# Gated sum of linear and softmax attention on one core: a new written-out order, later transposing loads, TensorE transposes in the last set, and split rings

## The chip, the cores and the metric

The kernel runs on one core of one Trainium2 chip. That core has TensorE (matmuls; PE in the profile, its weight loads PEld), VectorE (DVE), ScalarE (ACT), GpSimd (POOL) and SyncE (SP), which only issues DMA transfers here. The engines run beside each other and wait for each other with semaphores. The metric is the device time of one execution in microseconds (us); lower is better.

## What is computed

The input x has 2048 rows of 512 values. Branch A is linear attention with a learned feature map, branch B is plain softmax attention; both have 32 heads of 16. A sigmoid gate g mixes the two results row by row. Cut from the reference (weights `wqkv`, `w_phi`, `wo` are given per branch):

```python
# branch A
pq = einsum("bhsd,hdf->bhsf", q, w_phi);  pk = einsum("bhsd,hdf->bhsf", k, w_phi)
phi_q = concat([softmax(pq), softmax(-pq)]);  phi_k = concat([softmax(pk), softmax(-pk)])
kv = einsum("bhsf,bhsd->bhfd", phi_k, v);  z = einsum("bhsf->bhf", phi_k)
a = (einsum("bhqf,bhfd->bhqd", phi_q, kv) / (einsum("bhqf,bhf->bhq", phi_q, z)[..., None] + 1e-6)) @ wo_A
# branch B
p = softmax(einsum("bhqd,bhkd->bhqk", q, k) * 16 ** -0.5)
b = einsum("bhqk,bhkd->bhqd", p, v) @ wo_B
# gate
g = sigmoid((x * gate_w).sum(-1, keepdims=True));  out = g * a + (1 - g) * b
```

Branch B holds most of the work: 32 heads x 2048 x 2048 exponentials.

## The kernel before, in words

**Tiling.** x is held transposed in `xT` (512 channels on 4 x 128 partitions, 2048 columns). Branch B goes through 32 *sets*: a set is 512 query rows and 4 heads (8 heads share a group `g`, and `par` takes one half of them). In a set, each of the 16 key tiles `kt` (128 keys) gives two pieces of scores of 128 x 1024. TensorE makes each piece with two `qk` matmuls (L1067) into two of the seven PSUM banks of the ring `B_r`; the eighth bank, `psO`, gathers the result.

**Two engines take the exponentials.** Most key tiles go to ACT, which takes one piece of 128 x 1024 per instruction (L1077) into a buffer of the ring `E_r` (10 buffers). The others go to DVE, which makes an integer whose bits are an approximate exponential: four instructions of 128 x 512 (L1082) into part 0 of a buffer `T`, and then two *shifts* of 128 x 2048 (L1091) into parts 1 and 2 of the same buffer. A buffer of the ring `T_r` (3 of them) is thus one allocation of three parts. TensorE adds an ACT tile to `psO` with one `pv` round (four matmuls of 512 columns side by side, two for each piece, L1106), and a DVE tile with three rounds, whose weights are scaled copies of the values (`vB`, `vS`). Only tiles in `DSET` may go to DVE; of the last `ND(s)` (5) of them the planner decides one by one, during planning, to which engine each goes (`alt`, `choose`).

**After a set,** DVE empties `psO` into `OT` (L741), SP transposes it with a DMA (L1124) into `OTT`, DVE divides by the sums (L1128, L1129), and after two sets SP transposes the result (L1136) into `oBT`. The very last set uses four TensorE transposes (L1119) for the first of these steps and the DMA of L1136 for the second. The output projection (L1151) multiplies `oAT` and `oBT` by the two output weights; for the last 512 rows its last matmul is kept apart (L1156), since it needs the last set. DVE (L1167) or ACT (L1164) scales by 1 - g, and SP stores (L1170).

**Branch A and the projections** run in between: q, k and v of group g before its first set (L758, L813), the gate (L856, one-column matmuls), `Wp` (L874), sums of squares for a range check (`sumsq`, L886 and L889), and the feature map (`phi`) with its GpSimd sums (L946 to L956).

**What sets the order.** Nothing above is issued in the order of the source. `_build` records every operation with its engine, a priority (`st_(x)` is set number x on a nominal clock), a cost in us and its buffers (`add`). `_Sched.run` then plays these operations through a list scheduler, on the author's machine: at each step it places the operation that can start earliest, and on TensorE it weighs the next `qk` against other ready work with some tolerances (`_pick_pe`). `style(seed)` draws these tolerances, and the table `STYLES` holds one seed for each stretch of `WINDOW` us of the planned time. The result is one fixed list of instructions for each engine; each engine runs its list strictly in turn, and waits for semaphores where the plan says so. The planner's prices are fixed numbers: 0.905 for an ACT piece, 0.6 for a DVE instruction of L1082 or L1091, 5.0 for the issue of the transposing load `wat`.

**The start.** x arrives in two ways. Columns 0 to 1023 of `xT` come from two plain loads (`x_in`, L687) into `T` buffers, which TensorE transposes (L773) and ACT and DVE copy (L740, L741). Columns 1024 to 2047 come from two transposing DMA loads (L698). A third transposing load, `wat` (L700), brings a transposed weight.

Of the kernel before, what the change touches and what calls it, by code (L numbers as in the profile page):

```python
# [15 lines left out]
D = 512  # L16
# [12 lines left out]
DSET = (5, 7, 9, 11, 13, 15)  # L29
# [8 lines left out]
WINDOW = 20.0  # L38
STYLES = (0, 61504, 30715, 62437, 20893, 99383, 94218, 0, 0, 75239, 0, 42781, 82966, 0, 0, 54421, 94168, 4721, 53470, 5563, 49382, 0, 0, 57337, 54423, 7875, 0, 7940, 59810, 78070, 3529, 35308, 31287, 0, 22189, 0, 0, 16999, 0)
# [32 lines left out]
class _Op:  # L72
    __slots__ = ("eng", "fn", "occ", "lat", "prio", "deps", "tiles", "mode", "name", "dma", "lane", "kind",
                 "n_open", "users", "start", "end", "count", "sem", "vc", "seq", "est", "run", "alt", "frees")


class _Sched:
# [114 lines left out]
    def _pick_pe(self, cands, free, pend, last_mode):  # L192
# [3 lines left out]
        def due(o):  # L196
            return self.load(o.run, free, pend) - 0.5
# [17 lines left out]
        over = CONT if bc[1].kind == "cont" else (t - bc[1].est - PVS) if bc[1].kind == "pv" else min(t, self.nom) - bc[1].prio  # L215
# [185 lines left out]
def _general(fast):
# [197 lines left out]
def _build(ctx, nc, A_x, A_wqkv, A_w_phi, A_wo, B_wqkv, B_wo, gate_w, out):  # L599
# [100 lines left out]
    op_wat = add("sp", -90, 5.0, lambda e: e.dma_start_transpose(WAT[:], A_wqkv[:, 0:2 * D]), name="wat", dma=7.0)  # L700
# [549 lines left out]
```

## Time and profile before

| | |
|---|---|
| median of 3 runs | 773.16 us (772.70 to 773.52) |
| the profiled execution: its own time | 773.7 us |
| the same execution: span from first to last instruction | 771.8 us |
| busy in the span | ACT 710.9, DVE 703.8, PE 693.0, POOL 191.7 us |
| mean granted TensorE clock | 0.988 |
| exponentials | ACT 720 pieces (L1077); DVE 608 + 304 instructions (L1082, L1091) |

The span is 1.9 us shorter than the time of the same execution. A PE that is busy is not a PE at its peak, because matmuls overlap. An instruction's idle time stands in brackets with what ended it. In the views by stretches each engine has its busy time, with the number of instructions in brackets.

### The profile page before, as it was taken

Reading aid. Unit: us, or ns where it says so; the run is one execution under the profiler, and the core shown is the slowest. Engines: PE = TensorE matmul, PEld = TensorE weight load, DVE = VectorE, ACT = ScalarE, POOL = GpSimd, SP = SyncE. Lnnn points to the kernel's source line nnn. Section 1 sums busy time; section 2 is a strip of 40 time slices with the busy share of each in tenths; the row PEclk is TensorE's granted clock in tenths of the full one; section 3 lists DMA queues with packets and bytes.
Section 4 is the critical chain, followed back from the end, with each engine's and each line's share of the span. In section 5 each row is a group of like instructions: output and inputs, shape, how many; then the busy total and the mean of one; then the engine's idle time right before and its main releaser. Section 6 shows DMA issues by size and latency. Waiting matters only on the chain.

```text
span 771.8 us, 15551 instructions
## 1 busy us (share of the span) xinstructions
PE 693.0 (90%) x6390; PEld 218.9 (28%) x6452; DVE 703.8 (91%) x1228; ACT 710.9 (92%) x796; POOL 191.7 (25%) x226
## 2 busy tenths in 40 slices
PE   6999999999989999898999989998988998988883
PEld 3333333233323222232232222222222232222221
DVE  2887899999999999999999999999999999999991
ACT  3998798989999999999999999999999999999990
POOL 5216231233343432422232021222221121200000
PEclk9999899999999999999999999999999999999997
DMA  9200000001010000002122021120211211100001
GB/s 235 39 15 8 8 14 16 15 29 49 8 23 1 8 15 15 14 14 29 41 56 50 22 35 42 29 39 17 47 24 35 49 42 35 32 19 8 14 8 39
DMA packets 72702, 23.92 MB, mean 31 GB/s; under 512 B 64560, under 2 KB 72624, under 8 KB 72624
## 3 DMA queue, kind: packets, MB, share of 16 engines
q1 hardware_dynamic: 71568, 22.58, 13.8%
q8 instruction: 53, 0.87, 0.5%
q10 hardware_dynamic: 1056, 0.26, 0.2%
q14 instruction: 25, 0.20, 0.1%
HBM read 4.21 MB, written 2.10 MB: 8 GB/s over the span
## 4 chain that ended last, share of the span: by engine, by line
ACT 43%; PE 27%; DVE 24%; DMA 3%; SPq 1%; issue 1%; ACTq 0%
ACT E L1077 41%; DVE T L1082 13%; PE psR L1067 11%; PE psO L1106 7%; DVE T L1091 6%; PE psR L758 4%; PE psR L1151 2%; DMA OTT<-OT 2%; PE psR L813 1%; SPq L700 1%; ACT WAT L940 1%; DVE ob L1129 1%; DVE OT L741 1%; DMA oAT<-WAv 1%; DVE WAv L1167 1%
## 5 line engine op out<-in xcount | busy, mean ns | idle before, releaser
L1077 ACT ACTIVATE E<-psR 128x1024 bf16<-128x1024 f32 x720 | 678.1, 1057 | 30.2 <-PE psR L1067 21.0
L1082 DVE TENSOR_SCALAR T<-psR 128x512 int16<-128x512 f32 x608 | 387.9, 681 | 21.1 <-PE psR L1067 18.7
L1067 PE MATMUL psR<-qz,kT 64*128 64x512 bf16 x2048 | 348.5, 385 | 44.2 <-ACT E L1077 29.0
L1091 DVE TENSOR_SCALAR T<-T 128x2048 int16<-128x2048 int16 x304 | 199.4, 691 | 3.0
L1067 PEld LDWEIGHTS psR<-qz,kT 64*128 64x128 bf16 x2048 | 86.5, 93 | 301.8 <-ACT E L1077 179.3
L1106 PE MATMUL psO<-E,vB 128*18 128x512 bf16 x1440 | 132.0, 384 | 1.7 <-ACT E L1077 0.8
L1106 PE MATMUL psO<-T,vS 128*18 128x512 bf16 x1216 | 105.4, 383 | 0.5
L1106 PE MATMUL psO<-T,vB 128*18 128x512 bf16 x608 | 59.8, 384 | 1.5 <-DVE T L1082 1.3
L946 POOL TENSOR_TENSOR WAT<-WAT 128x512 f32<-128x512 bf16 x16 | 18.5, 1154 | 166.4 <-DVE T L1091 140.5
L1106 PEld LDWEIGHTS psO<-E,vB 128*18 128x18 bf16 x1440 | 33.0, 88 | 61.7 <-issue 41.5
L951 POOL TENSOR_TENSOR tr<-WAT 128x256 f32<-128x256 f32 x32 | 23.3, 728 | 79.3 <-DVE T L1091 79.3
L1106 PEld LDWEIGHTS psO<-T,vS 128*18 128x18 bf16 x1216 | 26.7, 87 | 57.4 <-DVE T L1091 26.6
L956 POOL TENSOR_TENSOR phk<-phk,ss 128x1024 bf16<-128x1024 bf16 x16 | 31.0, 1935 | 47.7 <-DVE T L1091 47.7
L956 POOL TENSOR_TENSOR WAT<-WAT,ss 128x1024 bf16<-128x1024 bf16 x16 | 30.9, 1928 | 46.3 <-DVE T L1091 46.3
L758 PE MATMUL psR<-xT,WB 128*128 128x512 bf16 x108 | 28.5, 380 | 4.1 <-issue 2.3
L758 PE MATMUL psR<-Wp,xT 128*128 128x512 bf16 x106 | 28.4, 380 | 3.4 <-issue 2.9
L946 POOL TENSOR_TENSOR WAT<-phk 128x512 f32<-128x512 bf16 x16 | 18.9, 1180 | 41.2 <-DVE T L1091 41.1
L741 DVE CAST OT<-psO 128x512 bf16<-128x512 f32 x32 | 21.8, 683 | 6.4 <-PE psO L1106 6.3
L1106 PEld LDWEIGHTS psO<-T,vB 128*18 128x18 bf16 x608 | 14.7, 87 | 31.3 <-issue 22.3
L826 POOL TENSOR_SCALAR vS<-vB 128x288 bf16<-128x288 bf16 x24 | 10.4, 433 | 51.1 <-DVE T L1091 48.4
L1129 DVE TENSOR_TENSOR ob<-OTT,rB 128x256 bf16<-128x256 bf16 x31 | 18.7, 604 | 0.2
L940 ACT ACTIVATE WAT<-psR 128x512 bf16<-128x512 f32 x32 | 18.3, 637 | 0.3 <-PE psR L758 0.3
(103 smaller groups left out, 372.2 us busy)
## 6 DMA issues: line engine op xcount, KB each, us to landing
qz<-qst SPq DMA_DIRECT2D x120, 16.0 KB, 1.8
out_dram<-WAv SPq DMA_DIRECT2D x12, 128.0 KB, 1.9
WB<-in_B_wqkv_dram SPq DMA_DIRECT2D x3, 384.0 KB, 6.7
T<-in_A_x_dram SPq DMA_DIRECT2D x2, 512.0 KB, 4.3
WAv<-in_A_wqkv_dram SPq DMA_DIRECT2D x1, 512.0 KB, 5.1
WB<-in_A_wo_dram SPq DMA_DIRECT2D x1, 512.0 KB, 3.5
WB<-in_B_wo_dram SPq DMA_DIRECT2D x1, 512.0 KB, 3.4
out_dram<-Wp SPq DMA_DIRECT2D x4, 128.0 KB, 3.8
```

The lines of the kernel that those rows point to most:

```text
L741: return add("dve", prio, 0.6, lambda e: e.tensor_copy(dst(), src()), deps=deps, tiles=tiles, name=name)
L758: calls = [lambda e, t=t: e.matmul(tile.ap[:, off:off + 512], lhsT=lhs(t), rhs=rhs(t), start=(t == 0), stop=(t == KT - 1)) for t in range(KT)]
L940: ex = [add("act", prio, 0.48, lambda e, s=s: e.activation(ev()[:, :, 16 * s:16 * s + 16], P(), ACTF.Exp, scale=1.0 - 2.0 * s), deps=[f] + ...
L946: p1 = pool(prio + 2, 1.23, lambda e: e.tensor_tensor(v8(), eg()[:, :, 0:8], eg()[:, :, 8:16], ALU.add), ex + use_wat, tiles=[ee, tr], nam ...
L951: p2 = pool(prio + 2, 0.92, lambda e: e.tensor_tensor(u4(), v8()[:, :, 0:4], v8()[:, :, 4:8], ALU.add), [p1], tiles=[tr, tr2])
L956: return pool(prio + 6, 1.95, lambda e: e.tensor_tensor(eg(), eg(), ss.ap[:, 1, :].unsqueeze(2).to_broadcast([128, 64, DH]), ALU.mult), [o ...
L1067: ins = e.matmul(rs[h].ap, lhsT=kT[64 * h:64 * h + 64, g, 128 * kt:128 * (kt + 1)], rhs=qt.ap[64 * h:64 * h + 64, c, :], start=True, stop= ...
L1077: exps.append(add("act", pr + 0.5 * cc, 0.905, lambda e, rs=rs, E=E: e.activation(E.ap.rearrange("p (a n) -> p a n", n=512), pair(rs), ACT ...
L1082: exps.append(add("dve", pr + 0.5 * cc + 0.01 * h, 0.6, lambda e, rs=rs, T=T, cc=cc, h=h: e.tensor_scalar(T.ap[:, 0, 1024 * cc + 512 * h:1 ...
L1091: s1, s2 = (add("dve", pr + 1.0 + 0.3 * m, 0.6, lambda e, T=T, m=m: e.tensor_single_scalar(T.ap[:, m, :], T.ap[:, 0, :], SHIFT[m], ALU.add ...
L1106: ins = e.matmul(O.ap[32 * col:32 * col + VW, :], lhsT=lhs(hd), rhs=rhs(cc)[:, 512 * h:512 * (h + 1)], start=(first_pv[s] == key), stop=(l ...
L1129: norm.append(add(eng, pr + 2, 0.33 if eng == "dve" else 0.7, lambda e, tv=tv, rb=rb, ob=ob, par=par: e.tensor_tensor(ob.ap.rearrange("p i ...
```

## The change: what it does

1. **Order.** `STYLES` has 181 seeds for stretches of 4 us, in place of 39 for stretches of 20. A seed now draws four more of the planner's weights (`lag`, `pref`, `pvs`, `stay`, `due`), from a generator written out in the file. Many priorities became constants at the top with other values; `ND` is 6 and `DSET` is (3, 5, ..., 13). The planner's prices are the same.
2. **Rings.** The buffer of three parts is split: `T_r` has 3 buffers of one part, and a new ring `TS_r` has 4, one for each shift. `E_r` has 12 buffers, `phk_r` 6.
3. **Start.** `wat` waits for the two transposing loads of x, so it stands behind them and behind the plain load of rows 512 to 1023. The first projections of k and q go matmul by matmul behind the four copies of `xT`.
4. **End.** In the last set, `psO` is emptied in two halves, and each half has its two transposes; the last transpose into `oBT` is made by TensorE (four transposes, one copy on DVE, one on ACT) and not by a DMA; `pv` of the last set has a higher priority than the output projections; ACT issues two of the last four stores.

Over the whole program ACT has 726 pieces (720 before), DVE 596 instructions of L1082's kind (608) and 298 shifts (304). TensorE changes between its three kinds of work (`qk`, `pv`, all else) 1084 times (1088).

```diff
-DSET = (5, 7, 9, 11, 13, 15)
+DSET = (3, 5, 7, 9, 11, 13)
...
+DUE, PREF = 0.5, 0.2
+GT = 2.2
+WP0 = 2.4
+CX0, CW0, CP0 = 1.2, 2.6, 3.4
+PK0, PK1 = 4.4, 0.5
+PQ0, PQ1, PQ2, PQ3 = 13.0, 0.75, 16.45, 0.95
+OF0 = 16.8
+NE_, NPH = 12, 6
-WINDOW = 20.0
-STYLES = (0, 61504, 30715, 62437, 20893, 99383, 94218, 0, 0, 75239, 0, 42781, 82966, 0, 0, 54421, 94168, 4721, 53470, 5563, 49382, 0, 0, 57337, 54423, 7875, 0, 7940, 59810, 78070, 3529, 35308, 31287, 0, 22189, 0, 0, 16999, 0)
+WINDOW = 4.0
+STYLES = (
+    0, 0, 0, 382076, 683899, 331868, 616951, 747786, 975194, 206425, 415652, 664137, 877502, 846153, 497104, 0, 66677, 207993, 0,
...
-ND = lambda s: 5
+ND = lambda s: 6
...
-        bq = min(qks, key=lambda c: (max(c[0], due(c[1])), c[1].seq)) if qks else None
+        bq = min(qks, key=lambda c: (max(c[0], due(c[1])) + (self.pref if c[1].run == "dve" else 0.0), c[1].seq)) if qks else None
...
+            self.lag, self.pref, self.pvs = r.uniform(2.0, 9.0), r.uniform(0.0, 0.4), r.uniform(2.0, 6.0)
+            self.stay, self.due = r.uniform(1.5, 5.0), r.uniform(0.3, 0.8)
...
-    E_r = ring(10, [128, 1024], name="E")
-    T_r = ring(3, [128, 3, 2048], I16, name="T")
-    phk_r = ring(4, [128, 1024], name="phk")
+    E_r = ring(NE_, [128, 1024], name="E")
+    T_r = ring(3, [128, 2048], I16, name="T")
+    TS_r = ring(4, [128, 2048], I16, name="TS")
+    phk_r = ring(NPH, [128, 1024], name="phk")
...
-    op_wat = add("sp", -90, 5.0, lambda e: e.dma_start_transpose(WAT[:], A_wqkv[:, 0:2 * D]), name="wat", dma=7.0)
+    op_wat = add("sp", -90, 5.0, lambda e: e.dma_start_transpose(WAT[:], A_wqkv[:, 0:2 * D]), deps=op_x23, name="wat", dma=7.0)
...
-                s1, s2 = (add("dve", pr + 1.0 + 0.3 * m, 0.6, lambda e, T=T, m=m: e.tensor_single_scalar(
-                    T.ap[:, m, :], T.ap[:, 0, :], SHIFT[m], ALU.add), deps=exps, tiles=[T], name="sh", kind="sh", alt=alt) for m in (1, 2))
+                s1, s2 = (add("dve", pr + 1.0 + 0.3 * m, 0.6, lambda e, T=T, X=X, m=m: e.tensor_single_scalar(
+                    X.ap, T.ap, SHIFT[m], ALU.add), deps=exps, tiles=[T, X], name="sh", kind="sh", alt=alt) for m, X in ((1, T1), (2, T2)))
...
-                o = add("pe", pr + 2.5, 0.22, pv, deps=list(dps) + [ev_v[g, kt // 4], op_psO] + more, tiles=holds + [O], mode="col",
+                o = add("pe", pr + 2.5 - 40.0 * (s == N_SETS - 1), 0.22, pv, deps=list(dps) + [ev_v[g, kt // 4], op_psO] + more, tiles=holds + [O], mode="col",
...
         if end:
-            calls = [lambda e, ot=ot, tt=tt, i=i: e.transpose(tt.ap.bitcast(BF16)[:, 128 * i:128 * (i + 1)],
-                                                              ot.ap[:, 128 * i:128 * (i + 1)], ident[:]) for i in range(4)]
-            n2 = chain(pr + 1.5, calls, 0.11, [n1, op_id], [ot, tt, rb, ob], "tpb")
+            n2 = None
+            for half in range(2):
+                sl = slice(256 * half, 256 * half + 256)
+                n1 = add("dve", pr - 3, 0.33, lambda e, ot=ot, O=O, sl=sl: e.tensor_copy(ot.ap[:, sl], O.ap[:, sl]), deps=pvs, tiles=[O, ot], name="Oev")
+                calls = [lambda e, ot=ot, tt=tt, i=i: e.transpose(tt.ap.bitcast(BF16)[:, 128 * i:128 * (i + 1)],
+                                                                  ot.ap[:, 128 * i:128 * (i + 1)], ident[:]) for i in (2 * half, 2 * half + 1)]
+                n2 = chain(pr - 20, calls, 0.11, [n1, op_id, n2], [ot, tt, rb, ob], "tpb")
...
+        if par == 1 and end:
             oBt = obt[qc]
-            op_oBT[qc, g] = add("sp", pr + 3, 1.3, lambda e, ob=ob, oBt=oBt, g=g: e.dma_start_transpose(
+            op_oBT[qc, g] = []
+            for half in range(2):
+                m = _Tile(M_r)
+                calls = [lambda e, i=i, half=half, m=m, ob=ob: e.transpose(m.ap.bitcast(BF16)[:, 128 * i:128 * (i + 1)],
+                                                                           ob.ap[:, 2 * half + i, :], ident[:]) for i in range(2)]
+                f = chain(pr - 20, calls, 0.11, norm + [op_id], [m, ob], "obt")
...
-        outs.append(add("sp", prio + 1, 0.63, lambda e, dst=dst, st=st: e.dma_start(out[0, 128 * st:128 * (st + 1), :], dst()),
+        outs.append(add("act" if last and i % 2 else "sp", prio + 1, 0.63, lambda e, dst=dst, st=st: e.dma_start(out[0, 128 * st:128 * (st + 1), :], dst()),
```

**SP's list at the start of the program**, before (line numbers of the kernel before):

```order
L687 DMA T<-in_A_x_dram 128x4x512
L677 DMA WB<-in_B_wqkv_dram 128x4x128
L677 DMA WB<-in_B_wqkv_dram 128x4x384 x3
L700 DMA_TRANSPOSE WAT<-in_A_wqkv_dram 128x8x512
L687 DMA T<-in_A_x_dram 128x4x512
L677 DMA WAv<-in_A_wqkv_dram 128x4x512
L677 DMA gw<-in_gate_w_dram 128x1 x4
L677 DMA Wbd<-in_A_w_phi_dram 16x4x16 x3
L698 DMA_TRANSPOSE xT<-in_A_x_dram 128x4x512 x2
```

and after the change (L716 is `x_in`, L727 the transposing loads of x, L729 `wat`):

```order
L716 DMA T<-in_A_x_dram 128x4x512
L706 DMA WB<-in_B_wqkv_dram 128x4x128
L706 DMA WB<-in_B_wqkv_dram 128x4x384 x3
L706 DMA WAv<-in_A_wqkv_dram 128x4x512
L706 DMA gw<-in_gate_w_dram 128x1 x3
L716 DMA T<-in_A_x_dram 128x4x512
L706 DMA gw<-in_gate_w_dram 128x1
L706 DMA Wbd<-in_A_w_phi_dram 16x4x16 x7
L727 DMA_TRANSPOSE xT<-in_A_x_dram 128x4x512 x2
L706 DMA Wbd<-in_A_w_phi_dram 16x4x16
L729 DMA_TRANSPOSE WAT<-in_A_wqkv_dram 128x8x512
```

`wat` moved from in front of the second plain load of x to the end of the loads. That load now has the plain load `WAv` and three loads of the gate's weight ahead of it.

**TensorE's list at the start**, before (L773 transposes x, L758 and L813 project, L1067 is `qk`, L1106 `pv`):

```order
L773 MATMUL psR<-ident,T 128x128 x16
L758 MATMUL psR<-xT,WB 128x512 x8
L813 MATMUL psR<-WB,xT 128x128 x16
L1067 MATMUL psR<-qz,kT 128x512 x4
L773 MATMUL psR<-ident,T 128x128 x16
L1067 MATMUL psR<-qz,kT 128x512 x2
L1106 MATMUL psO<-E,vB 18x512 x4
L1067 MATMUL psR<-qz,kT 128x512 x2
L758 MATMUL psR<-xT,WB 128x512 x4
L813 MATMUL psR<-WB,xT 128x128 x16
```

and after (L808, L787, L849, L1106 and L1143 are the same five):

```order
L808 MATMUL psR<-ident,T 128x128 x16
L787 MATMUL psR<-xT,WB 128x512 x8
L849 MATMUL psR<-WB,xT 128x128 x16
L808 MATMUL psR<-ident,T 128x128 x4
L1106 MATMUL psR<-qz,kT 128x512 x4
L808 MATMUL psR<-ident,T 128x128 x8
L1106 MATMUL psR<-qz,kT 128x512 x2
L808 MATMUL psR<-ident,T 128x128 x4
L1106 MATMUL psR<-qz,kT 128x512 x4
L1143 MATMUL psO<-E,vB 18x512 x4
L1106 MATMUL psR<-qz,kT 128x512 x4
L787 MATMUL psR<-xT,WB 128x512 x4
```

The transposes of the second block are now cut in three, and the first four of them stand ahead of the first `qk`.

**TensorE's list at the end of the program**, from the last `qk` on, before:

```order
L1067 MATMUL psR<-qz,kT 128x512 x4
L1106 MATMUL psO<-E,vB 18x512 x4
L1106 MATMUL psO<-T,vB 18x512 x4
L1151 MATMUL psR<-WB,oAT 128x512 x8
L1151 MATMUL psR<-WB,oBT 128x512 x6
L1151 MATMUL psR<-WB,oAT 128x512 x8
L1151 MATMUL psR<-WB,oBT 128x512 x6
L1106 MATMUL psO<-T,vS 18x512 x8
L1106 MATMUL psO<-E,vB 18x512 x4
L1119 MATMUL psR<-ident,OT 128x128 x4
L1156 MATMUL psR<-WB,oBT 128x512 x4
```

and after (L1205 is L1151's output projection, L1210 is L1156, L1159 is L1119, L1180 is the new transpose):

```order
L1205 MATMUL psR<-WB,oAT 128x512 x4
L1143 MATMUL psO<-TS,vS 18x512 x4
L1143 MATMUL psO<-E,vB 18x512 x4
L1205 MATMUL psR<-WB,oBT 128x512 x3
L1159 MATMUL psR<-ident,OT 128x128 x2
L1205 MATMUL psR<-WB,oAT 128x512 x4
L1159 MATMUL psR<-ident,OT 128x128 x2
L1205 MATMUL psR<-WB,oBT 128x512 x3
L1205 MATMUL psR<-WB,oAT 128x512 x4
L1180 MATMUL psR<-ident,ob 128x128 x4
L1205 MATMUL psR<-WB,oBT 128x512 x3
L1210 MATMUL psR<-WB,oBT 128x512 x3
```

Before, 28 matmuls of the output projections stand ahead of the last three `pv` rounds; now four of them do, and the others fill the room between the steps that follow. Behind the rows shown come four and three more matmuls of L1205 and the last one of L1210.

More of the change, by code (lines that the diff above doesn't have):

```diff
@@ L73, with __init__, uniform @@
     __slots__ = ("eng", "fn", "occ", "lat", "prio", "deps", "tiles", "mode", "name", "dma", "lane", "kind",
-                 "n_open", "users", "start", "end", "count", "sem", "vc", "seq", "est", "run", "alt", "frees")
+                 "n_open", "users", "start", "end", "count", "sem", "vc", "seq", "est", "run", "alt")
+class _Random:
+    def __init__(self, seed):
+        self.x = (seed * 0x9E3779B97F4A7C15 + 1) % 2 ** 64
+    def uniform(self, a, b):
+        self.x = (self.x * 6364136223846793005 + 1442695040888963407) % 2 ** 64
+        return a + (b - a) * ((self.x >> 11) / 2.0 ** 53)
 class _Sched:
@@ L196, in due @@
         def due(o):
-            return self.load(o.run, free, pend) - 0.5
+            return self.load(o.run, free, pend) - self.due
         qks = self._streams(cands, free, pend)
@@ L207, in _pick_pe @@
         if near:
-            bc = min(near, key=lambda c: (c[1].prio - (20.0 if c[1].kind == "cont" else 0.0) + (0.0 if c[1].mode == last_mode else 3.0) + 4.0 * (c[0] - t), c[1].seq))
+            bc = min(near, key=lambda c: (c[1].prio - (20.0 if c[1].kind == "cont" else 0.0) + (0.0 if c[1].mode == last_mode else self.stay) + 4.0 * (c[0] - t), c[1].seq))
         if bq is None:
@@ L397 @@
 T0 = 10.5
+XT1, TAIL = T0 + 0.5, None
 N_SETS = 32
@@ L916, in gsum @@
         return ins
[L917 to L919 removed]
+    g1 = add("pe", st_(GT + 0.1), 0.25, gsum, deps=[g0, op_ones], tiles=[mg], mode="full", name="gsum", nb=st_(GT - 0.4))
+    cert.append(add("dve", st_(GT + 0.1), 0.13, lambda e: e.tensor_copy(ct[:, 6:7], mg.ap[:, 0:1]), deps=[g1], tiles=[mg]))
+    pc = st_(max(CX0, CW0, CP0) + 3.0)
     c1 = add("dve", pc, 0.15, lambda e: e.tensor_reduce(ct[:, 8:9], ct[:, 0:4], AX.X, ALU.max), deps=cert)
@@ L1157, in _build @@
         fi = _Tile(fin_r) if not last else None
-        f1 = chain(prio, calls, MM, [op_oAT[st], op_woA, op_woB] + [op_oBT[qc, g] for g in range(KT - last)] + (tail_qk if last else []),
+        f1 = chain(prio, calls, MM, [op_oAT[st], op_woA, op_woB] + [x for g in range(KT - last) for x in op_oBT[qc, g]] + (tail_qk[:TAIL] if last else []),
                    [tile, oT, oBt] + ([fi] if fi else []), "of", prio - EARLY)
-        f2 = f1 if not last else add("pe", prio + 0.5, MM, second, deps=[f1, op_oBT[qc, KT - 1]], tiles=[tile, oT, oBt], mode="full",
+        f2 = f1 if not last else add("pe", prio - 20, MM, second, deps=[f1, op_oBT[qc, KT - 1][i // 2]], tiles=[tile, oT, oBt], mode="full",
                                      name="os")
```

151 lines of the change are left out of this document (80 added, 71 removed), and 10 rows, old and new, of the table STYLES.

## The prediction

> **What bounds the kernel now.** I read the busy times of the page first, then the busy times by stretches, then the list of waits.
>
> ```profile
> PE 693.0 (90%) x6390; PEld 218.9 (28%) x6452; DVE 703.8 (91%) x1228; ACT 710.9 (92%) x796; POOL 191.7 (25%) x226
> ...
> ACT 43%; PE 27%; DVE 24%; DMA 3%; SPq 1%; issue 1%; ACTq 0%
> ```
>
> Three engines are busy for 90% or more, and the chain that ended last runs through all three. The stretches (length, then busy us of PE, PEld, DVE, ACT, POOL, the granted clock, the DMA share and GB/s) tell more:
>
> ```profile
> 11.20:21.60 10.40, 5.79 (x49) 3.44 (x50) 2.09 (x6) 5.64 (x8) 5.63 (x3) 0.84 1.01 222
> 21.60:40.00 18.40, 16.73 (x157) 5.71 (x156) 16.30 (x27) 17.56 (x20) 3.94 (x7) 1.00 0.11 23
> 40.00:80.00 40.00, 38.20 (x379) 14.29 (x382) 34.36 (x56) 36.60 (x40) 15.95 (x14) 1.00 0.05 11
> 80.00:130.00 50.00, 48.01 (x466) 18.25 (x472) 44.86 (x84) 40.90 (x44) 12.37 (x13) 0.93 0.04 10
> 130.00:400.00 270.00, 248.78 (x2303) 76.65 (x2328) 257.96 (x442) 260.44 (x299) 90.90 (x106) 1.00 0.10 22
> 400.00:752.00 352.00, 318.92 (x2947) 93.12 (x2968) 342.31 (x604) 345.57 (x384) 55.92 (x61) 1.00 0.16 31
> ```
>
> Length less busy time is idle time. ACT idles 4.8 us in the first row and 0.8, 3.4, 9.1, 9.6 and 6.4 in the others: 34.1 in all, 29.3 of it after 21.6 us, which I call its middle idle. DVE idles 8.3 and then 2.1, 5.6, 5.1, 12.0 and 9.7: 42.9, of which 34.6 in the middle. Both finish together:
>
> ```profile
> 741.65 10.33 ACT L1077 ACTIVATE E<-psR 128x1024 bf16<-128x1024 f32 x11
> ...
> 750.50 1.29 DVE L1091 TENSOR_SCALAR T<-T 128x2048 int16<-128x2048 int16 x2
> ```
>
> ACT's last exponential ends at 752.0, DVE's last shift at 751.8. I call this moment X. So the two engines that share the exponentials are the bound together, from 11.2 us to X. What they wait for in between:
>
> ```profile
> ACT E L1077 <- PE psR L1067: 21.0, 49, 1.8
> ...
> ACT E L1077 <- PE psO L1106: 7.0, 7, 2.0
> ```
>
> Mostly it is the next `qk`; 7.0 us in seven waits is for a `pv` that must free a buffer of `E_r`. Behind X lie 771.8 - 752.0 = 19.8 us of ending. The profiled execution took 773.7, thus 1.9 more than its span; the median of the runs is 0.5 below it.
>
> **More pieces on ACT, fewer on DVE.**
>
> ```profile
> L1077 ACT ACTIVATE E<-psR 128x1024 bf16<-128x1024 f32 x720 | 678.1, 1057 | 30.2 <-PE psR L1067 21.0
> L1082 DVE TENSOR_SCALAR T<-psR 128x512 int16<-128x512 f32 x608 | 387.9, 681 | 21.1 <-PE psR L1067 18.7
> ...
> L1091 DVE TENSOR_SCALAR T<-T 128x2048 int16<-128x2048 int16 x304 | 199.4, 691 | 3.0
> ```
>
> Neighbours overlap, so I divide busy time by count: 678.1/720 = 0.942 for a piece on ACT, 387.9/608 = 0.638 and 199.4/304 = 0.656 on DVE. Six more pieces cost ACT 6 x 0.942 = **+5.7**. Twelve and six fewer instructions give DVE 12 x 0.638 + 6 x 0.656 = **-11.6**.
>
> **The start.**
>
> ```profile
> 3.58 8.10 SPq L700 DMA_TRANSPOSE WAT<-in_A_wqkv_dram  x1
> ...
> 5.93 1.06 PE L773 MATMUL psR<-ident,T 128*128 128x128 bf16 x16
> ...
> 10.78 0.65 PE L1067 MATMUL psR<-qz,kT 64*128 64x512 bf16 x4 [0.28 <-DVE qz L807]
> ...
> 11.21 1.94 ACT L1077 ACTIVATE E<-psR 128x1024 bf16<-128x1024 f32 x2 [1.85 <-PE psR L1067]
> 11.73 0.58 SPq L687 DMA_DIRECT2D T<-in_A_x_dram  x1
> ...
> 15.88 1.89 PE L773 MATMUL psR<-ident,T 128*128 128x128 bf16 x16 [4.45 <-DMA T<-in_A_x_dram]
> ...
> 21.88 2.47 DVE L1082 TENSOR_SCALAR T<-psR 128x512 int16<-128x512 f32 x4
> ```
>
> The issue of `wat` holds SP for 8.10 us, though the planner prices it at 5.0; the second load of x goes out at 11.73 and lands at 15.88. ACT and DVE have that block's copies in their lists, so they stand still. In the new list the load waits only for the first one (which had landed when the transposes began at 5.93), but the bytes ahead of it are more:
>
> ```profile
> WB<-in_B_wqkv_dram SPq DMA_DIRECT2D x3, 384.0 KB, 6.7
> T<-in_A_x_dram SPq DMA_DIRECT2D x2, 512.0 KB, 4.3
> WAv<-in_A_wqkv_dram SPq DMA_DIRECT2D x1, 512.0 KB, 5.1
> ...
> WB<-in_B_wqkv_dram ACTq DMA_DIRECT2D x2, 128.0 KB, 5.1
> ```
>
> ```profile
> 3.00:13.00 10.00, 7.43 (x53) 3.74 (x51) 3.28 (x8) 3.60 (x6) 5.56 (x14) 1.00 1.18 300
> ```
>
> With the third load of 128 KB on SP these are 3 x 384 + 2 x 512 + 512 + 3 x 128 = 3072 KB, or 3.1 MB. From 3 us on at 300 GB/s they take 10.4: an estimate of 13.2 for the landing, 2.7 earlier than before. But the new TensorE list has four transposes of this block ahead of the first `qk`. They take 0.3 (a quarter of 1.06), and ACT's first piece began 0.4 after its `qk` (10.78 to 11.21); so ACT begins at 13.7, not at 11.2: 2.5 later. Against that the 4.8 of idle go: **-2.2** for ACT. Bounds: if the load lands before 11 us, nothing is late and the gain is 4.8; if it lands at 15.88 as before, ACT starts 5.2 later and the term is +0.4. For DVE, key tile 3 is in the set now and needs only the first block, so its first exponential moves from 21.88 to about 15: **-6.9** (0, if its `qk` come no sooner).
>
> `wat` itself now follows at about 21 and holds SP until about 29. Behind it stand the copies of q for the second group, first needed in the third set; a set lasts 740/32 = 23 us, so this costs nothing.
>
> **The middle, the large unknown.** With the middle idle as it is, ACT would end at 752.0 - 2.2 + 5.7 = 755.5, DVE at 751.8 - 11.6 - 6.9 = 733.3. The same planner, with the same prices, gave tiles to the two engines so that they ended 0.2 apart. I take it that they end together again, at the mean: X = **744.4**. Then ACT's middle idle falls by 11.1 to 18.2, and DVE's grows by as much. In favour: two more `E_r` buffers go against the 7.0 us; a less loaded DVE gives back PSUM banks sooner; the last row shows that ACT can run with 1.8% idle (6.4/352). Against: TensorE is not relieved, it has the same matmuls but for 24 of `pv`, and in the row from 80 to 130 us it is busy for 48.0 of 50. So I stay at the mean. The bounds are 755.5 (nothing falls) and 733.3 (ACT waits no longer than DVE lets it).
>
> **The end.**
>
> ```profile
> 751.29 1.68 PE L1151 MATMUL psR<-WB,oAT 128*128 128x512 bf16 x7 [0.16 <-issue]
> ...
> 757.21 0.61 PE L1106 MATMUL psO<-T,vS 128*18 128x512 bf16 x8
> ...
> 758.84 0.40 PE L1119 MATMUL psR<-ident,OT 128*128 128x128 bf16 x4 [0.80 <-DVE OT L741]
> ...
> 762.47 1.09 PE L1156 MATMUL psR<-WB,oBT 128*128 128x512 bf16 x4 [3.24 <-DMA oBT<-ob]
> ...
> 763.70 0.68 ACT L1164 ACTIVATE Wp<-psR,omg 128x512 bf16<-128x512 f32 x1
> ...
> L1170 SPq DMA_DIRECT2D out_dram<-Wp x4: 353/436/1727, 763.7 to 765.0; - x4
> ```
>
> Before, the last `pv` stand behind 28 matmuls of the projection until 757.21, and after the transposes TensorE waits 3.24 for a DMA. The last store goes out at 765.0, 6.8 before the span's end. In the new list I add up TensorE from X on: 0.2 until it starts, 0.6 for eight matmuls of `pv`, 28 projection matmuls of (757.21 - 751.29)/27 = 0.22 (6.1), eight transposes of 0.10 (0.8): the last matmul ends at X + 7.7. The copies on DVE and ACT in between lie beside projection matmuls. Then 0.7 for the last scaling on ACT, 0.1 to the store, and the same 6.8: X + 15.3, or **-4.5**. If TensorE waits at each of the seven hand-overs for 0.2, it is -3.0; I allow as much the other way, -6.0.
>
> The Trainium skill speaks against the transposes on TensorE ("TensorE: Matmul & The Clock Gate", Part 4: PE-mode transpose): about 275 ns each inside a kernel. By that the eight would take 2.2 and the sum would end 1.4 higher, at 762.5. The trace does not agree: it shows four in 0.40 us.
>
> **Sum.** 744.4 + 15.3 + 1.9 - 0.5 = **761.1**.
>
> **Rivals.** (a) *The new order saves nothing in the middle.* The planned order rests on prices that the chip doesn't keep (0.6 against 0.638 on DVE), and each short stretch may be fitted to them. Then ACT sets the end: 755.5 + 15.3 + 1.4 = 772.2, no change. Against it: seven waits have a cause that the larger ring takes away. Chance 0.11. (b) *TensorE becomes the bound, and it is slower.* Between 80 and 130 us ACT idles 18%, while the one-column gate matmuls, `Wp` and the sums of squares crowd TensorE and the clock falls to 0.93. If the new order crowds 80 us more of the stretch to 400 us like that, ACT idles 80 x (0.18 - 0.035) = 11.6 more than in (a): 783.8. It decides from 2.5 us more idle than before. For it: the new list still runs the gate's matmuls as one cluster; against it: the count of changes between kinds of work is the same (1084). Chance 0.07. (c) *The middle idles everywhere as little as the last row,* 1.8% of 730 us, 13.3, or less: X = 739.5, 756.2, with 749 to 757 as its range. Chance 0.18. (d) *The load does not come sooner,* because the queue is full: the term becomes +0.4, 763.7. Chance 0.06.
>
> **How the numbers follow.** The forecast has 0.58; its own range is 754 to 768, from the ends of the start (-2.6 to +2.6), of the end (1.5 each way) and about half the way to either bound of the middle. Below 751 I leave 0.05, above 772 about 0.1: the range is 751 to 772. A change under 0.2% (1.5 us) can't be told from none here. (a) gives half its chance to faster; forecast, (c) and (d) are faster: 0.87. The rest of (a) is no change, 0.06; (b) is slower, 0.07.
>
> **What would show it.** Start: the second x load issued at about 6 and landed near 13, first ACT piece near 13.7, DVE's first L1121 near 15, and no ACT gap of 3.8 behind it. Middle: ACT idle after 22 us near 18 in place of 29.3, waits on `pv` well under 7.0, DVE idle near 46. End: last exponential near 744, first L1210 matmul about 5 later, 15.3 from X to the span's end. I am wrong if ACT's middle idle stays at 29 or grows, or if the two engines end far apart.

## The result and the profile after

The changed kernel takes **749.78 us** (median, 749.46 to 750.14) beside 773.34 us for the kernel before, run next to it: a ratio of 0.9689, with a 95% interval from 0.9666 to 0.9712. The forecast was 761.1 with a range of 751 to 772. The sign was right; the change brought 23.6 us where 12.1 were forecast, and the time lies below the range. Of the rivals, (c), 749 to 757, came nearest.

First the page of the profile after: the span, then the busy time of the engines, then the chain that ended last by engine.

```profile
span 747.6 us, 15606 instructions
...
PE 695.1 (93%) x6432; PEld 216.0 (29%) x6432; DVE 693.4 (93%) x1212; ACT 711.6 (95%) x803; POOL 193.7 (26%) x234
...
ACT 65%; PE 26%; DVE 5%; DMA 2%; SPq 1%; issue 0%; DVEq 0%
```

ACT has the same 711 us of work as before (710.9) in a span 24 us shorter, and its share of the chain went from 43% to 65%. ACT is now closer to being the bound alone. The same stretches as in the prediction, of the kernel after; the last two rows are cut at its own X, 734.3:

```profile
11.20:21.60 10.40, 7.90 (x50) 2.75 (x50) 5.67 (x10) 6.25 (x8) 0.83 (x3) 0.67 0.72 152
21.60:40.00 18.40, 18.20 (x190) 6.98 (x186) 17.61 (x29) 17.51 (x21) 3.34 (x7) 1.00 0.27 58
40.00:80.00 40.00, 39.14 (x422) 14.52 (x418) 35.73 (x61) 38.38 (x42) 24.63 (x20) 1.00 0.07 15
80.00:130.00 50.00, 49.15 (x474) 17.48 (x475) 46.10 (x85) 45.74 (x51) 10.59 (x13) 0.97 0.05 12
130.00:400.00 270.00, 252.42 (x2372) 77.02 (x2372) 260.26 (x452) 266.01 (x306) 93.09 (x108) 1.00 0.10 23
400.00:734.30 334.30, 312.46 (x2844) 89.81 (x2840) 321.48 (x564) 332.98 (x373) 54.21 (x60) 1.00 0.16 32
734.30:747.60 13.30, 7.04 (x44) 3.15 (x40) 3.14 (x7) 1.75 (x3) 0.00 (x0) 0.96 0.14 45
```

Length less ACT's busy time, row by row from 21.6 us to X: 0.9, 1.6, 4.3, 4.0 and 1.3 (before: 0.8, 3.4, 9.1, 9.6 and 6.4). The middle idle of ACT is 12.1 us, and not 29.3. DVE's is 31.5 (34.6 before). In the last row but one ACT stands still for 0.4% of the time. TensorE is busy for 312.46 of 334.30 there, 93.5% (before 318.92 of 352, 90.6%).

The waits of the exponentials (what waited for what: us in total, times, longest), and the groups of instructions they belong to:

```profile
ACT E L1116 <- PE psR L1106: 15.8, 28, 5.4
...
DVE T L1121 <- PE psR L1106: 16.3, 45, 1.5
```

```profile
L1116 ACT ACTIVATE E<-psR 128x1024 bf16<-128x1024 f32 x726 | 679.8, 1120 | 17.2 <-PE psR L1106 15.8
L1121 DVE TENSOR_SCALAR T<-psR 128x512 int16<-128x512 f32 x596 | 380.8, 683 | 20.8 <-PE psR L1106 16.3
```

ACT's pieces wait 28 times for `qk` and never for a `pv` that has to free a buffer of E (before: 49 times, and 7.0 us in seven waits for `pv`). The 5.4 is the wait at the start. The moment X and the end, from the timeline (start, duration, engine, line; the idle time before it in brackets):

```profile
723.00 11.29 ACT L1116 ACTIVATE E<-psR 128x1024 bf16<-128x1024 f32 x12
...
731.91 1.30 DVE L1129 TENSOR_SCALAR TS<-T 128x2048 int16<-128x2048 int16 x2
...
738.80 0.81 PE L1210 MATMUL psR<-WB,oBT 128*128 128x512 bf16 x3
...
740.96 0.38 PE L1210 MATMUL psR<-WB,oBT 128*128 128x512 bf16 x1
741.38 0.69 ACT L1218 ACTIVATE Wp<-psR,omg 128x512 bf16<-128x512 f32 x1 [1.25 <-PE psR L1210]
742.09 0.41 ACTq L1224 DMA_DIRECT2D out_dram<-Wp  x1
```

X is 734.3 on ACT and 733.2 on DVE. So 17.7 of the 24.2 us of span lie ahead of X, and 6.5 behind it: the ending is 13.3 long in place of 19.8. For ACT the 17.7 are 17.2 of middle idle and 0.6 of idle at the start, less 0.2 of busy time more: almost the whole gain ahead of X is waiting that is gone.

### The profile page after: what moved, and what is told of

It is laid out like the page before. It is cut to its first block, busy times and chain, and to the rows that moved or that the text cites. A ratio compares the mean times of both kernels' runs of the same rounds, so it can differ in the third digit from the quotient of the medians.

```text
span 747.6 us, 15606 instructions
## 1 busy us (share of the span) xinstructions
PE 695.1 (93%) x6432; PEld 216.0 (29%) x6432; DVE 693.4 (93%) x1212; ACT 711.6 (95%) x803; POOL 193.7 (26%) x234
## 4 chain that ended last, share of the span: by engine, by line
ACT 65%; PE 26%; DVE 5%; DMA 2%; SPq 1%; issue 0%; DVEq 0%
ACT E L1116 62%; PE psR L1106 10%; PE psO L1143 6%; PE psR L787 4%; PE psR L1205 3%; DVE T L1121 2%; PE psR L849 2%; ACT WAT L979 2%; ACT phk L979 1%; DMA OTT<-OT 1%; DVE TS L1129 1%; SPq L706 1%; DMA T<-in_A_x_dram 1%; PE psR L927 1%; DVE ob L1170 1%
## 5 line engine op out<-in xcount | busy, mean ns | idle before, releaser
L1116 ACT ACTIVATE E<-psR 128x1024 bf16<-128x1024 f32 x726 | 679.8, 1120 | 17.2 <-PE psR L1106 15.8
L1121 DVE TENSOR_SCALAR T<-psR 128x512 int16<-128x512 f32 x596 | 380.8, 683 | 20.8 <-PE psR L1106 16.3
L1106 PE MATMUL psR<-qz,kT 64*128 64x512 bf16 x2048 | 347.5, 386 | 38.3 <-ACT E L1116 28.0
L1129 DVE TENSOR_SCALAR TS<-T 128x2048 int16<-128x2048 int16 x298 | 193.2, 684 | 3.1
L1106 PEld LDWEIGHTS psR<-qz,kT 64*128 64x128 bf16 x2048 | 87.0, 93 | 306.6 <-ACT E L1116 221.3
L1143 PE MATMUL psO<-E,vB 128*18 128x512 bf16 x1452 | 127.1, 382 | 0.0
L1143 PE MATMUL psO<-TS,vS 128*18 128x512 bf16 x1192 | 105.6, 382 | 0.6 <-DVE TS L1129 0.6
L1143 PE MATMUL psO<-T,vB 128*18 128x512 bf16 x596 | 58.7, 384 | 0.0
L990 POOL TENSOR_TENSOR tr<-WAT 128x256 f32<-128x256 f32 x32 | 23.4, 733 | 94.5 <-DVE TS L1129 94.5
L1143 PEld LDWEIGHTS psO<-E,vB 128*18 128x18 bf16 x1452 | 31.3, 88 | 51.3 <-issue 37.1
L1143 PEld LDWEIGHTS psO<-TS,vS 128*18 128x18 bf16 x1192 | 26.6, 87 | 53.3 <-issue 29.5
L787 PE MATMUL psR<-Wp,xT 128*128 128x512 bf16 x128 | 33.2, 382 | 0.8 <-DVE T L1121 0.8
L787 PE MATMUL psR<-xT,WB 128*128 128x512 bf16 x128 | 33.2, 382 | 0.4 <-ACT WAT L979 0.2
L985 POOL TENSOR_TENSOR WAT<-phk 128x512 f32<-128x512 bf16 x16 | 18.7, 1166 | 31.2 <-DVE TS L1129 31.2
L1143 PEld LDWEIGHTS psO<-T,vB 128*18 128x18 bf16 x596 | 14.5, 87 | 27.9 <-issue 21.4
L862 POOL TENSOR_SCALAR vS<-vB 128x144 bf16<-128x144 bf16 (+1 forms) x32 | 11.9, 373 | 39.4 <-DVE TS L1129 34.0
L979 ACT ACTIVATE phk<-psR 128x512 bf16<-128x512 f32 x32 | 18.6, 675 | 0.8 <-PE psR L787 0.8
```

What stands on the lines that cost most here:

```text
L787: calls = [lambda e, t=t: e.matmul(tile.ap[:, off:off + 512], lhsT=lhs(t), rhs=rhs(t), start=(t == 0), stop=(t == KT - 1)) for t in range(KT)]
L979: ex = [add("act", prio, 0.48, lambda e, s=s: e.activation(ev()[:, :, 16 * s:16 * s + 16], P(), ACTF.Exp, scale=1.0 - 2.0 * s), deps=[f] + ...
L985: p1 = pool(prio + 2, 1.23, lambda e: e.tensor_tensor(v8(), eg()[:, :, 0:8], eg()[:, :, 8:16], ALU.add), ex + use_wat, tiles=[ee, tr], nam ...
L990: p2 = pool(prio + 2, 0.92, lambda e: e.tensor_tensor(u4(), v8()[:, :, 0:4], v8()[:, :, 4:8], ALU.add), [p1], tiles=[tr, tr2])
L1106: ins = e.matmul(rs[h].ap, lhsT=kT[64 * h:64 * h + 64, g, 128 * kt:128 * (kt + 1)], rhs=qt.ap[64 * h:64 * h + 64, c, :], start=True, stop= ...
L1116: exps.append(add("act", pr + 0.5 * cc, 0.905, lambda e, rs=rs, E=E: e.activation(E.ap.rearrange("p (a n) -> p a n", n=512), pair(rs), ACT ...
```

## The experiments

Line numbers differ a little from kernel to kernel; the names of the tiles are the same. "Lists kept" means: the planned lists of the kernel after, in which only the named instructions are moved. I give the ratio to the kernel before, run on the same chip, with its 95% interval. All twelve runs are told.

**Take away the seeds.** In the kernel after, and in the kernel before:

```diff
-STYLES = (0, 0, 0, 382076, ...)
+STYLES = ()
```

> The kernel after, with an empty table of seeds: the planner uses its default weights throughout; rings, priorities, start and end are those of the change. Theory S (the search in short stretches removed the idle time of the middle): ACT's middle idle goes back to 25 us or more and the time is 763 to 775 us. Rival R (the larger and split rings and the new priorities removed it, whatever the weights): ACT's middle idle stays below 16 us and the time is 749 to 756 us.

> The kernel before, with an empty table of seeds. It says what its 39 seeds for stretches of 20 us were worth, and gives the partner for the kernel after without seeds. Theory S: seeds matter in the kernel before too, 778 to 790 us. Rival R: 771 to 776 us.

The kernel after without seeds took 772.21 us, a ratio of 0.9976 (0.9964 to 0.9987): nearly the whole gain is gone. The kernel before without its seeds took 788.75, 1.0196 (1.0167 to 1.0225). Waits of the kernel after without seeds, its ACT pieces, and its stretch from 21.6 to its own X (756.2); behind it the same stretch of the kernel before without seeds (X 766.6):

```profile
ACT E L1105 <- PE psR L1095: 29.2, 58, 4.9
ACT E L1105 <- PE psO L1132: 5.3, 2, 2.8
...
DVE T L1110 <- PE psR L1095: 33.7, 68, 1.6
```

```profile
L1105 ACT ACTIVATE E<-psR 128x1024 bf16<-128x1024 f32 x726 | 682.3, 1065 | 35.8 <-PE psR L1095 29.2
```

```profile
21.60:756.20 734.60, 680.44 (x6288) 206.91 (x6280) 682.10 (x1186) 703.43 (x788) 185.26 (x206) 1.00 0.12 26
```

```profile
21.60:766.60 745.00, 682.89 (x6316) 207.76 (x6313) 699.55 (x1217) 700.11 (x781) 179.62 (x198) 1.00 0.12 25
```

The lists of the kernel after without seeds hold the same work (726 pieces on ACT, 596 and 298 instructions on DVE), on the same rings, with the same ending. In the full table 142 of the 182 entries are seeds; a 0 stands for the plain weights, and the first three entries are 0 (in the kernel before 26 of 39 are seeds). Without the search the waits of both engines for `qk` are about twice as long, and the middle idle is 734.60 - 703.43 = 31.2 on ACT and 52.5 on DVE. The search, then, does not move waiting from one engine to the other: it takes it away from both.

**The rings, without seeds.** The kernel after without seeds, with the rings of before (E in 10 buffers, T and its shifts in 3 buffers of three parts, phk in 4):

> The kernel after without seeds (default weights, as a_noseed with 772.2 us), planned with the rings of before: 10 buffers of E, 3 buffers of three parts for T and its shifts, 4 of phk. Theory (the split and larger rings give room even at default weights): 775 to 780 us. Rival (rings matter only for a searched order, or not at all): 770 to 773 us.

775.74 us, 1.0011 (1.0000 to 1.0021), beside 0.9976 with the new rings: at the planner's plain weights the rings are worth 0.35% of the time, about 3 us. Its stretch up to its X:

```profile
21.60:759.90 738.30, 684.15 (x6315) 208.66 (x6307) 690.52 (x1198) 699.47 (x785) 185.89 (x206) 1.00 0.12 26
```

What is then left between this kernel and the kernel before without seeds, 1.85% or 14 us, is in the constants, the shares of the engines, the start and the end.

**The number of E buffers under the searched lists.** Lists kept; the buffers of E are dealt again, each to the next user when it comes free first, over 10 buffers, and as a control over 12:

```diff
+    reassign([E_r], e_tiles, 10)   # control: 12
+    retime()
```

> The kernel after with its lists kept, and the pieces of ACT dealt to 10 buffers of E in place of 12 (each piece takes the buffer that came free first in the plan). Theory (the order leans on all twelve): ACT waits for pv again, 1 to 6 us in all, and the time is 751 to 756 us. Rival (twelve give only slack): 749 to 750.5 us.

> A control for the run with E in 10 buffers (770.7): the lists of the kernel after are kept, and the 12 buffers of E are dealt again by the same rule (the buffer that comes free first goes to the next user). If the number of buffers is what cost 20.9: 749.8 within 2. If the new dealing cost it: 760 or more.

With 10 it took 770.69 us, 0.9949; with 12 it took 748.05, 0.9662 (0.9634 to 0.9690), as the kernel after. The dealing costs nothing, and the two missing buffers cost 21 to 23 us (against the kernel after and against the control) where I had expected 1 to 6. Waits with 10:

```profile
ACT E L1123 <- PE psO L1150: 23.4, 22, 2.0
ACT E L1123 <- PE psR L1112: 13.8, 25, 5.7
```

ACT now waits 23.4 us for `pv` to free a buffer. The searched lists let `pv` trail ACT so far that they need the last two buffers again and again. That does not make the rings the cause of what the change gained: a search that knows of 10 buffers finds other lists, as the next runs show.

**A search of my own on three structures.** A beam search of the same kind, over stretches of 4 us, but with a small effort: six orders kept, six new ones tried for each. On the kernel after, on the kernel after with the rings of before, and on the kernel before in all its parts:

```diff
-WINDOW = 20.0          # in the kernel before; 4.0 in the kernel after
+WINDOW = 4.0
-STYLES = (...)
+STYLES = (... the seeds found for this structure ...)
```

> The kernel after with other seeds: a beam search of my own over the same 4 us stretches, with a small effort (6 orders kept, 6 new ones tried for each). Theory S (short searched stretches are what emptied the middle): well below the 772.2 of the kernel after without seeds, about halfway to the 749.8 of its own seeds, 757 to 764; the exponentials on ScalarE wait less than the 29.2 on TensorE's scores and 5.3 on the products that they took without seeds. Rival L (the gain hangs on those very seeds and a search of this kind gives little): 768 to 773.

> The kernel after with the rings of before (E in 10 buffers, T and its two shifted copies in 3 buffers of three parts, phk in 4) and seeds of the same small beam search, run for this structure. Theory S: the search works as well on these rings, so it stands above the kernel with the new rings and the same search by what the rings gave without seeds (775.7 less 772.2), 2 to 6 us: 760 to 768. Rival R (the rings are what lets the search work; ScalarE waits on the products for a buffer of E): it gains under 5 us on its 775.7 without seeds, 771 to 776, with more than 10 us of waits of E on the products.

> The kernel before in all its parts, with seeds of the same small beam search over 4 us stretches in place of its 39 seeds over 20 us. Its 39 seeds were worth 788.75 less 773.3, about 15. Theory S (short searched stretches do it): the search gives more than those 15: 763 to 771. Rival R (without the new rings, priorities, start and end the search is stuck): 771 to 778, no better than the seeds that it had.

They took 761.70 us, 0.9842 (0.9814 to 0.9871); 767.44, 0.9921 (0.9892 to 0.9950); and 769.69, 0.9943 (0.9924 to 0.9961). All three times are within what theory S gave. For each the last exponentials of ACT (and of DVE, where it ends later), and the stretch from 21.6 to the later of the two ends, in the order told; behind the second its waits of E on the products:

```profile
734.27 8.56 ACT L1122 ACTIVATE E<-psR 128x1024 bf16<-128x1024 f32 x9
...
745.71 1.29 DVE L1135 TENSOR_SCALAR TS<-T 128x2048 int16<-128x2048 int16 x2
```

```profile
21.60:747.00 725.40, 679.26 (x6304) 207.96 (x6302) 688.84 (x1193) 700.61 (x787) 186.52 (x206) 1.00 0.13 26
```

```profile
737.42 8.54 ACT L1123 ACTIVATE E<-psR 128x1024 bf16<-128x1024 f32 x9
...
750.31 1.29 DVE L1136 TENSOR_SCALAR T<-T 128x2048 int16<-128x2048 int16 x2
```

```profile
21.60:751.60 730.00, 682.46 (x6325) 209.51 (x6322) 690.05 (x1198) 699.18 (x784) 184.89 (x206) 1.00 0.12 26
```

```profile
ACT E L1123 <- PE psO L1150: 5.3, 5, 1.4
```

```profile
21.60:748.00 726.40, 677.26 (x6309) 209.31 (x6307) 684.41 (x1199) 703.69 (x788) 179.42 (x198) 1.00 0.12 25
```

In the first two DVE ends 4.2 and 5.6 us behind ACT: the small search didn't bring the two engines to one end, as the other lists do within 2 us. That time counts as idle time of ACT here. The middle idle in us up to the later end, each from a row shown (length less busy time; before and after as the sums of their rows):

| kernel | ACT | DVE | both |
|---|---|---|---|
| before, no seeds | 44.9 | 45.4 | 90.3 |
| before, its 39 seeds | 29.3 | 34.6 | 63.9 |
| before, my small search | 22.7 | 42.0 | 64.7 |
| after with the old rings, no seeds | 38.8 | 47.8 | 86.6 |
| after with the old rings, my small search | 30.8 | 40.0 | 70.8 |
| after, no seeds | 31.2 | 52.5 | 83.7 |
| after, my small search | 24.8 | 36.6 | 61.4 |
| after | 12.1 | 31.5 | 43.6 |

A small search takes 22 us of idle out of the kernel after, and the seeds of the change take 40. The last 18 of these lie between two tables of seeds on the very same structure, so they are the order alone (the two differ in two pieces, 724 on ACT and 726). On the old rings the small search works too, if less: it takes 16 us of idle and 0.9% off the 1.0011 without seeds, and a further 0.8% comes with the new rings, where without seeds they gave 0.35%. So the larger part of the middle is the search and the smaller part the rings. That each is worth more with the other is what the medians say, but this difference of two differences, 0.4%, is no larger than its own uncertainty, and each structure had one search only, which has its luck. On the kernel before the small search does better than its 39 seeds by 0.57%.

**The ending of before.** The kernel after, with the last set and the four stores written as before; the lists up to the last set are the same:

> The kernel after, with the ending of before: pv of the last set without the raised priority, one copy out of psO, a transposing DMA into oBT, all four last stores on SP. The lists up to the last set are the same. Theory: the way from the last exponential to the end grows from 13.3 us back to about 19.8, time 756.3 us (755 to 757.5). Rival: half of that is hidden since the projections stand elsewhere in the list, 752 to 754 us.

755.16 us, 0.9755 (0.9728 to 0.9781), beside 0.9689: the new ending is worth 5 us. From its timeline:

```profile
732.24 3.04 ACT L1116 ACTIVATE E<-psR 128x1024 bf16<-128x1024 f32 x3
...
742.35 1.19 SPq L1174 DMA_TRANSPOSE oBT<-ob  x1
744.82 1.89 PE L1194 MATMUL psR<-WB,oBT 128*128 128x512 bf16 x4 [3.25 <-DMA oBT<-ob]
...
746.24 3.22 SPq L1208 DMA_DIRECT2D out_dram<-Wp  x4
```

The 3.25 us that TensorE waited for the transposing DMA before are back, and four stores on SP hold it for 3.22. X is 735.3 and the span 753.9, so the way from X to the end is 18.6 us, near the 19.8 of before.

**The start.** Three runs with the lists kept: `wat` ahead of the second x load, as before (`WAv` and the gate's weight `gw` go behind it); the second x load ahead of the weight `WAv` and of `gw` on SP; and, beside that, the first two `qk` ahead of the four transposes of this second block on TensorE.

```diff
+    move("sp", op_wat, xin[1])
+    # second run, in its place
+    move("sp", xin[1], [o for o in sch.order["sp"] if o.name == "wav"][0])
+    # third run, beside the second
+    for o in q1:
+        move("pe", o, x1)
```

> The kernel after with its lists kept, but on SP the transposing load wat stands ahead of the second plain load of x again, and WAv and the gate's weight behind that. The second load of x should land near 15.9 us in place of 13.6, and the four transposes ahead of the first qk hold ACT's first piece until about 17. Theory (ACT's work is the bound from its first piece on, so a late start is paid in full): 751.5 to 752.5 us. Rival (the start is hidden, since later idle time takes it up): 749.3 to 750.3 us.

> The kernel after with its lists kept, but on SP the second plain load of x goes out ahead of WAv and of the gate's weight. In the kernel after it was issued at 7.59 and landed at 13.6, TensorE stood still for 3.8 us, and the granted clock was 0.50 from 13 to 18 us. Theory (the start is paid in full, and the clock falls because of that gap): the load is issued near 6 and lands near 11.3, the gap shrinks to about 1.5 us, the clock stays at 1.00, ACT's first piece moves from 14.87 to about 12, and the time falls by 2.5 to 4 us, to 746 to 747.5. Rival (later idle time takes it up): 749 to 750.

> As a_x1_first, and on TensorE the first two qk stand ahead of the first four transposes of the second block, so that ACT's first piece need not wait for that load. Theory: ACT's first piece near 10.7, a further 0.5 to 1.3 us less than a_x1_first: 745 to 746.5. Rival: no further change, since the next pieces wait for the copies of that block anyway.

With `wat` early: 751.51 us, 0.9699 (0.9669 to 0.9728), and the first piece of ACT at 17.41; the medians are 1.7 apart, but its interval overlaps with that of the change, so the time decides for neither theory nor rival. With the load first: 746.43, 0.9635 (0.9617 to 0.9653). That is the expected time, but not quite by the expected way: TensorE's gap was 2.55 us and not 1.5, the clock fell all the same, and ACT's first piece came at 13.09 and not near 12. With the two `qk` as well: **745.52, 0.9623** (0.9605 to 0.9641), the fastest kernel of this study, 4 to 5 us faster than the change (by the medians and by the ratios). The second and the third can't be told apart by their intervals. In their traces ACT's first piece starts 2.4 us sooner in the third, but its last piece ends only 0.4 sooner (first the run with the load first, then the one with the two `qk` as well), so what these two `qk` add is open:

```profile
698.90 32.36 ACT L1116 ACTIVATE E<-psR 128x1024 bf16<-128x1024 f32 x35
```

```profile
699.41 31.46 ACT L1116 ACTIVATE E<-psR 128x1024 bf16<-128x1024 f32 x34
```

Now the kernel after at the start:

```profile
5.18 2.37 SPq L706 DMA_DIRECT2D gw<-in_gate_w_dram  x3
7.59 0.43 SPq L716 DMA_DIRECT2D T<-in_A_x_dram  x1
...
13.70 0.59 PE L808 MATMUL psR<-ident,T 128*128 128x128 bf16 x4 [3.77 <-DMA T<-in_A_x_dram]
...
14.87 1.02 ACT L1116 ACTIVATE E<-psR 128x1024 bf16<-128x1024 f32 x1 [5.42 <-PE psR L1106]
...
16.80 1.29 DVE L1121 TENSOR_SCALAR T<-psR 128x512 int16<-128x512 f32 x2
```

```profile
13.00:14.00 1.00, 0.30 (x4) 0.33 (x4) 0.00 (x0) 0.00 (x0) 0.19 (x1) 0.50 0.11 5
...
18.00:19.00 1.00, 1.00 (x8) 0.25 (x8) 0.78 (x3) 0.90 (x1) 0.00 (x0) 0.50 1.11 214
```

Then the third run:

```profile
5.31 0.37 SPq L716 DMA_DIRECT2D T<-in_A_x_dram  x1
...
10.64 1.02 ACT L1116 ACTIVATE E<-psR 128x1024 bf16<-128x1024 f32 x1 [1.20 <-PE psR L1106]
...
12.71 0.40 PE L808 MATMUL psR<-ident,T 128*128 128x128 bf16 x4 [0.30 <-DVE xT L770]
```

In the kernel after three tiny loads of `gw` hold SP for 2.37 us ahead of the second x load. TensorE then waits 3.77 us for it, and the granted clock falls to 0.50 in every row from 13 to 19 us: four transposes take 0.59. In the third run the load goes out at 5.31, TensorE has work while it comes, the clock stays at 1.00, four transposes take 0.40, and ACT's first piece starts 4.2 us sooner.

## Why the prediction was wrong, point by point

The forecast was too slow by 761.1 - 749.8 = 11.3 us: 10.1 in X, 2.0 in the end, and 0.8 the other way between the span and the median (2.2, forecast 1.4).

- **The failed step is "The middle, the large unknown".** There I let the two engines end together *at the mean* of 755.5 and 733.3, that is, I held the sum of their middle idle at 63.9 us and only dealt it out anew: 18.2 for ACT, 45.7 for DVE. That they end together was right (1.1 us apart). That the sum stays was wrong: it fell to 43.6, 12.1 on ACT and 31.5 on DVE. In the prediction's own terms X is the mean of the two engines' ends, so a sum that is 20.3 lower brings X 10.1 down: that is the whole miss in X, since the misses in the two terms below, about -2.4 for the pieces and +2.4 for the start in this mean, cancel by luck. The kernel without seeds shows a sum of 83.7 with the same work, and the small search on the same structure 61.4, so the sum is for the most part what the order makes of it. I had the sign of it in (c), where every stretch idles like the last row of before, and gave it 0.18. My argument against more was that TensorE is not relieved. It wasn't, but it was 90.6% busy in the last stretch and went to 93.5% with nearly the same work: it was not full. In us for ACT, the middle is 6.1 better than forecast (17.2 against 11.1).
- **More pieces on ACT**: forecast +5.7 on ACT and -11.6 on DVE. DVE's busy time from 11.2 us to X came out at -11.0 (its two groups alone at 574.0 - 587.3 = -13.3). ACT's busy time from 11.2 us to X grew by 0.2 only, 5.5 less than forecast. The 726 pieces together took 1.7 more, not 5.7, since one took 679.8/726 = 0.936 in place of 0.942, and ACT's other work took 1.0 less. A piece alone lasts 1.02 us, twelve in a row 11.29, which is 0.94 each, and there were half as many waits (28 for 56). The kernel after without seeds, with 60 waits, needed 682.3 us for the same 726 pieces, 2.5 more. So the fewer waits can account for the larger part of the 4.0 by which the price was too high; where the rest comes from is open.
- **The start**: forecast -2.2 for ACT; measured -0.6, so 1.6 worse. The direction and the size of the landing were right: the load landed at 13.7 (forecast 13.2). It was issued at 7.59 and not at about 6, behind the `gw` loads, whose issue I had not priced. The missed part lies behind the landing: ACT began 1.2 us after the landing and not 0.5, with TensorE at half its clock in between. (Two sums of that step are off as well: 3 + 10.4 is 13.4, not 13.2, and its own parts, 0.3 and 0.4, make 0.7 behind the landing, not 0.5.) The measured -0.6 belongs to one execution: in the run with the old ending, whose lists are the same up to the last set, ACT's first piece came at 14.89 too, but the mean clock of the row was 0.84 in place of 0.67, and ACT was busy for 6.71 in place of 6.25:

```profile
11.20:21.60 10.40, 7.58 (x54) 2.78 (x54) 6.13 (x12) 6.71 (x9) 0.83 (x3) 0.84 0.72 152
```

  The Trainium skill ("TensorE: Matmul & The Clock Gate", Part 1, "What's actually happening") says that the clock is halved after an idle window of about 3.4 us and comes back after a busy one; the gap of 3.77 and the clock of 0.50 agree. The run with the load first doesn't quite: there the clock fell too, in a gap of only 2.5 us, and here the measurement decides:

```profile
11.92 0.58 PE L808 MATMUL psR<-ident,T 128*128 128x128 bf16 x4 [2.55 <-DMA T<-in_A_x_dram]
```

```profile
12.00:13.00 1.00, 1.00 (x8) 0.37 (x7) 0.46 (x2) 0.00 (x0) 0.00 (x0) 0.50 1.09 176
```

  For DVE I forecast its first exponential at about 15 and -6.9; it came at 16.80, and the idle of its first row went from 8.3 to 4.7, -3.6. With `wat` put back the median rose by 1.7 us, near the 2.2 that I gave the step, although not told from nothing by its interval. That `wat` behind the loads costs nothing later was right: nothing on ACT, DVE or PE waits for it.
- **The end**: forecast 15.3, measured 13.3. The mechanism was right: `pv` first, transposes on TensorE, no wait for a DMA, and the run with the old ending loses 5 us. TensorE's last matmul ended 7.0 behind X (forecast 7.7). The term that was mis-sized is the last one: from the last store to the span's end I kept the 6.8 of before, and it is 5.5. Before, all four stores went out on SP, and the issue of the last one alone held it for 1.73 us (the largest in the prediction's line); now two go out on ACT, and the last issue takes 0.41. Behind that issue both kernels take 5 us to the end of the span. The four transposes at 0.10 each held too, 0.39 us for four.
- **The rivals.** (a) fell: the searched lists are planned with the same wrong prices and still work on the chip. (b) fell: between 80 and 130 us ACT idles 4.3, not 9.1, and the clock there rose from 0.93 to 0.97. (c) was nearest: the middle idles 12.1 of 712.7 us, 1.7% where it had 1.8%, though not everywhere alike as it said: 8.5% from 80 to 130 us and 4.1% from 40 to 80, but 0.4% in the last stretch. (d) fell: the load came 2.2 us sooner.

What stays open: which part of the search did it, the shorter stretches (4 us for 20), the four more weights that a seed draws (`pref`, `pvs`, `stay`, `due`; `lag` was drawn before too, from a smaller range) or the effort, was not tried apart; nor was a large search on the old rings. Of the 1.85% between the two kernels without seeds and with the same rings, the ending explains about 0.7%; how the rest is shared among the constants, the engines' shares and the start was not tried. Nor was the kernel before with 12 buffers of E.

## What to carry to other kernels

When two engines share a load and both wait for a third, the sum of their idle time isn't a given: ask what the order alone could take out, and find out by measuring the same kernel with a plain order (83.7 us of idle here, beside 43.6), before you hold it constant. A frozen order and its rings belong together: two buffers fewer cost some 22 us under lists that were searched for twelve, but only about 6 (with the smaller rings of T and phk as well) where the same small search was run on both. At the start of a kernel, put the load that the first work waits for ahead of those that are needed later, small ones too, and give TensorE something to do in between; both together brought 4 to 5 us here, most of it by the order of the loads.

## What the runs showed of the hardware

- The granted TensorE clock fell to 0.50 in gaps of 3.77 and of 2.55 us at the start, and stayed there until about 19.5 and 15 us; where the longest gap was 0.94 us it stayed at 1.00. How long it stays low is not fixed by the list: in the run with the old ending, the same list with a gap of 3.47 us, the clock was back between 16 and 17 us.
- The same transposing load `wat` held SP for 8.10 us when it was issued at 3.6 us, behind other loads, and for half as long when it was issued at 20.5:

```profile
20.47 4.17 SPq L729 DMA_TRANSPOSE WAT<-in_A_wqkv_dram  x1
```

- Three loads of one column of `gw` held SP for 2.37 us, 0.8 each, while the load of 512 KB of x behind them held it for 0.43. What an issue costs did not go by the bytes.
